# Query, key and value products of an attention block: eight block products or seven, head groups by pairs or segment by segment

## The chip, the cores and the metric

The kernel runs on one core of one Trainium2 chip. A core has five engines that work side by side, each through its own list of instructions in order: TensorE (matmuls, called PE in the profile, its weight loads PEld), VectorE (DVE), ScalarE (ACT), GpSimd (POOL) and SyncE (SP). SP here only issues transfers, which 16 DMA engines carry out. Operands lie in SBUF, an on-chip memory of 128 partitions; matmul results go to PSUM, which has eight banks of 128 x 512 floats. DRAM is outside. An engine waits for another through semaphores. The metric is the device time of one execution in microseconds, lower being better.

## What is computed

A transformer block on 2048 tokens of 1024 features: attention with a compressive memory, then a gated feed-forward, each behind a layer norm whose scale and shift come from a conditioning vector. Cut to what matters:

```python
h = _layernorm(x) * (1 + ca) + sa
q, k, v = h @ wq, h @ wk, h @ wv          # 32 heads of 32, four segments of 512 tokens
for s in range(4):
    p = softmax(qs @ ks.T * scale + causal_mask)      # within the segment
    a_dot = p @ vs
    a_mem = (phi(qs) @ M) / (phi(qs) @ z + 1e-6)      # memory of the segments before
    o = g * a_mem + (1 - g) * a_dot
    M, z = M + phi(ks).T @ vs, z + phi(ks).sum()
x = x + ga * (o @ wo)
h = _layernorm(x) * (1 + cb) + sb
x = x + gb * ((gelu(h @ w_gate) * (h @ w_up)) @ w_down)
```

## The kernel before

Every large product is made in three matmuls: both operands are cut into a high part, which a matmul takes in one pass, and a low part, the rest; high x high, high x low and low x high are added. A cut is one copy on ScalarE and one subtraction on VectorE or GpSimd.

The feed-forward (`gate_up`, L1034, and `down_seven`, L1205) already uses a scheme of seven products in place of eight: both operands are seen as 2 x 2 blocks, sums and differences of blocks are formed, and seven block products, added in the right way, give the four blocks of the result. Its combined weights (tiles `B`, 512 KB with high and low part) are made once, stored in the DRAM tensor `bc_d`, and loaded again for the later token passes (`b_load`, L994).

Attention goes in 32 steps, each for one group of four heads and one segment of 512 tokens. The list `steps` (L1410) takes segments 0 and 1 of all eight groups first, then segments 2 and 3, so that the weights of a group serve two steps. `weights` (L347) loads and cuts them; the normed, transposed tokens of two segments stay in SBUF (`hT_tile`, L73). Inside a step:

- `kv_part` (L423) makes keys and values in ordinary products, tokens by features: 96 matmuls of 256 columns. `k_out` (L386) turns the keys and copies them by three transfers into the stacked tile `ks`: the 128 partitions of four heads become 32 partitions times four, three times over (L395).
- `q_part` (L439) makes the queries in 24 matmuls of 512 columns, and three more transfers stack them in `qs` (L419).
- `scores` (L482) finds each row's maximum and sum: 16 matmuls, each with a VectorE and a ScalarE operation behind it. `sums` and `memory` (L466, L520) carry the memory forward and read it.
- `values` (L544), one step later, makes the transposed scores (`T`), their exponentials, and the product with the values, and stores 256 KB to `oT_d`.

TensorE's order is the program's throughout (`manual_schedule`, L1418), SP's at the start (L1419) and in the feed-forward (L1511); otherwise a planner orders each engine's instructions when the kernel is built, from costs that it assumes. All transfers leave through SP's one queue. The string `ORDER` (L1411) is the interleaving: its letters take one piece each from the generators of values (V), scores (S), memory sums and reads (A, M), keys and values of the next step (K), queries of the next step (Q) and the norm of later tokens (N). In the last steps K and Q stand for the output projection (`projections`, L675). `todo` lists weight loads and modulation rows by position. `first_part` (L450) makes the products of step 0 while the start is still loading.

Of the kernel before, what the change touches and what calls it, by code (L numbers as in the profile page):

```python
# [11 lines left out]
F32 = mybir.dt.float32  # L12
F32R = mybir.dt.float32r
AF = mybir.ActivationFunctionType
ALU = mybir.AluOpType
# [21 lines left out]
def block_kernel(ctx: ExitStack, tc: tile.TileContext, x, c, wmod, wq, wkv, wo, beta, wg, wu, wd, out):  # L37
# [21 lines left out]
    podd, podd_close = pool("podd", "left")  # L59
    pev, pev_close = pool("pev", "left")  # L60
    pw, pw_close = pool("pw", "left")
    pa, pa_close = pool("pa", "right")

# [3 lines left out]
    def wsp_tile(name):  # L67
        return pw.tile([P, 2, 1024], F32R, name=name, tag="wsp", bufs=5)
# [4 lines left out]
    def hT_tile(name, s):  # L73

        return (pev, podd)[s % 2].tile([P, L], F32R, name=name, tag="hT", bufs=16)
# [33 lines left out]
    raw0 = [fetch(wkv[0, 0], "k0"), fetch(wkv[0, 1], "v0"), fetch(wq[0], "q0")]  # L109
# [94 lines left out]

    def load_w(src, name):
        return split_w(fetch(src, name), wsp_tile("w" + name))
# [118 lines left out]
    def norm_seg(s, halves):  # L325
        hs = hT[s] = []
        for kt in range(KT):
            ps = s_ps(f"tpa{s}_{kt}")
            for i in range(4):
                nc.tensor.transpose(ps[:, i * P:(i + 1) * P], halves[kt // 4][i][:, (kt % 4) * P:(kt % 4 + 1) * P], ident)  # L330
            h = tmp_tile(f"h{s}_{kt}")
            nc.scalar.activation(h, ps, AF.Identity, bias=modT[:, kt:kt + 1], scale=modT[:, 8 + kt:9 + kt])
            hi = hT_tile(f"hha{s}_{kt}", s)
            lo = hT_tile(f"hla{s}_{kt}", s)
            nc.scalar.activation(hi, h, AF.Copy)  # L335
            nc.vector.tensor_sub(lo, h, f32(hi))  # L336
            hs.append((hi, lo))
            yield


    hT, W, Mst, ST, SC, PK = {}, {}, {}, {}, {}, {}
    ks_t = []
    for n in range(2):
        k = p1.tile([P, 4, L], F32R, name=f"ks{n}")
        ks_t.append(k)

    def weights(half, g, at):  # L347

        W[g] = [None] * 3
        raws = [None] * 3  # L350

        def get(i):
            raws[i] = fetch((wq[g], wkv[g, 0], wkv[g, 1])[i], f"{i}_{half}_{g}")

        def cut(i):
            W[g][i] = split_w(raws[i], wsp_tile(f"w{i}_{half}_{g}"))

        for pos, f, i in at:
            todo.append((pos, lambda f=f, i=i: (get, cut)[f](i)))

    def kv_mm(ps, g, s, t, kt, **kw):
        hi, lo = hT[s][kt]
# [1186 lines left out]
```

## Time and profile before

| | |
|---|---|
| median of three runs | 2916.93 us (2914.0 to 2917.47) |
| the profiled execution | 2917.27 us, its span 2915.5 us |
| start, to the end of the first products | 0 to 52 us |
| the stretch of the attention products | 52 to 984 us |
| last steps and output projection | 984 to about 1202 us |
| feed-forward | 1202 to 2915 us |
| matmuls of keys and values (L366) | 3072 of 256 columns |
| matmuls of queries (L372) | 768 of 512 columns |
| bytes moved in all | 682.97 MB |

The profile gives busy times per engine; a "chain" follows the last instruction back through what released each step; a table by windows gives busy time, granted TensorE clock, the share of time that the 16 DMA engines were taken, and the rate. For a group of instructions a row holds the line, the engine, the operation, result <- operands, the shape, the count, the busy time in us, the mean duration of one in ns, and the idle time ahead of it. A matmul's duration is its latency; matmuls overlap, so what one costs is read from the distance of their starts, or from a run of them in the chain.

### The profile page before, as it was taken

What the parts mean: (1) busy time and instruction counts of PE and PEld (TensorE: products, weight loads), DVE (VectorE), ACT (ScalarE), POOL (GpSimd) and SP (SyncE); (2) the same over time, 40 slices, a digit from 0 to 9 for tenths busy, and PEclk for the clock granted to TensorE, in tenths of its full rate; (3) what the DMA queues carried; (4) which work ended last, traced back from release to release, by engine and by line L of the source; (5) the groups of instructions that cost most, each with busy time, mean ns of one, the idle gap of its engine ahead of it and who ended that gap; (6) DMA issues with size and microseconds to landing.
All of it is one profiled execution on the core that took longest, in us unless ns stands there. A gap on an engine that the chain in (4) does not pass through costs nothing.

```text
span 2915.5 us, 48821 instructions
## 1 busy us (share of the span) xinstructions
PE 2833.7 (97%) x17248; PEld 2532.0 (87%) x17248; DVE 1860.2 (64%) x4293; ACT 1263.5 (43%) x3112; POOL 882.6 (30%) x1428
## 2 busy tenths in 40 slices
PE   5999999999999999999999999999999999999999
PEld 4788887888888778899999999899999998999998
DVE  7566566766666824656666666756666685666667
ACT  6677776776666624355433333221222122221221
POOL 0333334433343423544455443112211111111111
PEclk9999999999999999999999999999999999999999
DMA  7557656666555648778888776988877788777775
GB/s 241 110 124 138 149 112 132 146 134 121 108 114 95 165 158 263 285 276 307 296 312 322 306 262 242 377 315 308 314 290 281 281 332 308 283 286 289 289 289 210
DMA packets 236053, 682.97 MB, mean 234 GB/s; under 512 B 23712, under 2 KB 62624, under 8 KB 225312
## 3 DMA queue, kind: packets, MB, share of 16 engines
q1 hardware_dynamic: 235808, 679.85, 72.0%
q8 instruction: 136, 2.23, 0.3%
q14 instruction: 109, 0.89, 0.1%
HBM read 454.32 MB, written 175.11 MB: 216 GB/s over the span
## 4 chain that ended last, share of the span: by engine, by line
PE 76%; DVE 8%; DMA 6%; ACT 4%; issue 3%; POOL 2%; SPq 0%; DVEq 0%; POOLq 0%; ACTq 0%
PE f L1043 32%; PE kv L366 9%; PE d L1286 7%; PE y L627 4%; PE q L372 3%; PE T L557 3%; PE db L1223 2%; PE da L1223 2%; PE ds L1223 2%; PE dc L1223 2%; PE S L493 2%; PE O L566 2%; ACT sj L497 2%; DMA B<-bc_d 1%; PE dd L1223 1%
## 5 line engine op out<-in xcount | busy, mean ns | idle before, releaser
L1043 PE MATMUL f<-A,B 128*128 128x320 f32 (+1 forms) x7056 | 1118.3, 319 | 15.7 <-DMA B<-bc_d 9.3
L1043 PEld LDWEIGHTS f<-A,B 128*128 128x128 f32 x7056 | 1104.3, 188 | 24.9 <-DVE c L1055 6.2
L495 DVE CUSTOM_DVE_ANT_0 sj<-S,mask 128x384 f32<-128x384 f32 (+3 forms) x512 | 229.6, 487 | 227.2 <-PE S L493 208.8
L497 ACT ACTIVATE sj<-sj,mm 128x384 f32<-128x384 f32 (+3 forms) x512 | 281.4, 551 | 114.7 <-DVE mm L495 114.4
L789 POOL TENSOR_TENSOR rt<-rt 128x256 f32<-128x256 f32 x104 | 79.0, 781 | 739.6 <-DMA rt<-wd 656.5
L560 POOL TENSOR_SCALAR_AFFINE_SELECT pt<-pt 128x128 f32<-128x128 f32 x512 | 171.0, 355 | 340.2 <-ACT pt L559 334.4
L1286 PE MATMUL d<-wd,hc 128*128 128x512 f32 x1128 | 260.2, 390 | 1.9 <-DVE hc L1106 1.3
L1286 PEld LDWEIGHTS d<-wd,hc 128*128 128x128 f32 x1128 | 211.0, 188 | 46.3 <-DVE hc L1106 2.0
L366 PE MATMUL kv<-w,hha 128*128 128x256 f32 x1024 | 207.4, 288 | 3.4 <-ACT hha L335 3.4
L366 PE MATMUL kv<-w,hhh 128*128 128x256 f32 x1024 | 201.6, 285 | 0.0
L559 ACT ACTIVATE pt<-T 128x256 f32<-128x256 f32 (+3 forms) x512 | 181.7, 456 | 39.0 <-PE T L557 34.4
L202 POOL TENSOR_TENSOR w<-r,w 128x256 fp32r<-128x256 f32 x180 | 133.0, 769 | 166.7 <-ACT w L197 166.5
L366 PEld LDWEIGHTS kv<-w,hha 128*128 128x128 f32 x1024 | 170.0, 195 | 4.7 <-ACT hha L335 4.3
L1115 ACT ACTIVATE hc<-g 128x256 fp32r<-128x256 f32 (+2 forms) x182 | 78.2, 443 | 212.3 <-DVE acc L1232 124.0
L1066 ACT ACTIVATE g<-g 128x320 f32<-128x320 f32 (+1 forms) x84 | 41.1, 489 | 292.3 <-DVE g L1065 292.3
L366 PEld LDWEIGHTS kv<-w,hhh 128*128 128x128 f32 x1024 | 166.4, 191 | 0.3 <-issue 0.2
L1312 DVE TENSOR_TENSOR acc<-acc,d 128x512 f32<-128x512 f32 x176 | 118.8, 684 | 57.5 <-PE d L1286 56.3
L557 PEld LDWEIGHTS T<-qs,ks 128*128 128x128 f32 x512 | 81.2, 191 | 84.7 <-issue 35.1
L366 PE MATMUL kv<-w,hla 128*128 128x256 f32 x512 | 147.6, 288 | 6.8 <-DVE hla L336 6.3
L557 PE MATMUL T<-qs,ks 128*128 128x256 f32 (+2 forms) x512 | 128.6, 361 | 20.2 <-DVE qs L510 7.6
L366 PE MATMUL kv<-w,hlh 128*128 128x256 f32 x512 | 144.9, 283 | 0.0
L1053 ACT ACTIVATE c<-f 128x320 f32<-128x320 f32 (+1 forms) x84 | 38.2, 455 | 236.6 <-PE f L1043 236.6
(246 smaller groups left out, 5247.9 us busy)
## 6 DMA issues: line engine op xcount, KB each, us to landing
B<-bc_d SPq DMA_DIRECT2D x392, 512.0 KB, 6.8
bc_d<-B SPq DMA_DIRECT2D x196, 512.0 KB, 6.7
wd<-wc_d SPq DMA_DIRECT2D x54, 1024.0 KB, 8.1
wc_d<-wd SPq DMA_DIRECT2D x28, 1024.0 KB, 8.0
rt<-wd SPq DMA_DIRECT2D x54, 512.0 KB, 7.5
ks<-kh SPq DMA_DIRECT2D x64, 256.0 KB, 5.6
qs<-qh SPq DMA_DIRECT2D x64, 256.0 KB, 7.3
wm<-wmod SPq DMA_DIRECT2D x32, 512.0 KB, 5.1
```

What stands on the lines that cost most here:

```text
L202: eng.tensor_sub(w[:, 1, k:k + 256], r[:, k:k + 256], f32(w[:, 0, k:k + 256]))
L366: nc.tensor.matmul(ps, b[:, sl], w[:, a], start=(kt == 0 and a == 0 and b is hi), stop=(kt == KT - 1 and a == 1), **kw)
L495: nc.vector.tensor_tensor_reduce(out=sj[:, :nv], in0=ps[:, :nv], in1=mask[:, L - nv:], scale=-1.0, scalar=3.4e38, op0=ALU.add, op1=ALU.min ...
L497: nc.scalar.activation(sj[:, :nv], sj[:, :nv], AF.Exp, bias=mm[:, j, i:i + 1], scale=-1.0, accum_out=ll[:, i, j:j + 1])
L557: nc.tensor.matmul(ps[:, :nn], ks[:, j, kc * P:(kc + 1) * P], qs[:, j, L - nn:], start=True, stop=True)
L559: nc.scalar.activation(pt, ps[:, nn - n:nn], AF.Exp)
L560: nc.gpsimd.affine_select(pt[:, :P], pt[:, :P], pattern=[[1, P]], compare_op=ALU.is_ge, fill=0.0, base=0, channel_multiplier=-1)
L627: nc.tensor.matmul(ps, b[:, i * P:(i + 1) * P], w[:, a, g % 2], start=(g == 0 and a == 0 and b is hi), stop=(g == G - 1 and a == 1))
L1043: nc.tensor.matmul(ps, B[m, i][:, a, kt * P:(kt + 1) * P], A[p, i, kt][b], start=(start and kt == 0 and a == 0 and b == 0), stop=(kt == 3 ...
L1223: nc.tensor.matmul(ps, t[:, c:c + P], B(a), start=(start and a == 0 and b == 0), stop=(stop and a == 1), skip_group_check=True)
L1286: nc.tensor.matmul(ps, hid[m][:, b, tt * P:(tt + 1) * P], down_w[m][:, a, nb * L:(nb + 1) * L], start=(m == chunks[0] and a == 0 and b == ...
L1312: nc.vector.tensor_add(dst, dst, ps)
```

## The change

Attention goes segment by segment: all eight groups of segment 0, then of segment 1 and so on, in alternating order of the groups, so that the last group's weights of one segment serve the first step of the next. Queries and keys of a group are one product of tokens by [wq | wk], values of four groups another; each is done in seven block products, with the two halves of the 512 tokens and of the 1024 features as blocks of the one operand, and of the weights as blocks of the other. The first value products and groups 0 and 1 of segment 0 remain ordinary ones.

```diff
+    ad_d = dram.tile([(NSEG - 1) * 7 * P, 4 * L], F32, name="ad_d")
+    bq_d = dram.tile([G * 7 * P, 2 * L], F32, name="bq_d")
+    bv_d = dram.tile([4 * 7 * P, 2 * L], F32, name="bv_d")
...
+    NB = 9
+    PRODUCTS = (1, 6, 2, 7, 5, 4, 3)
```

The weight combinations of a unit are made once (`make`), each cut and stored as a 512 KB tile; the six units that segment 0 needs next go straight into the pool of nine tiles as well. Afterwards `pump` loads them back in the order of the list `lq`, one for each tile released:

```diff
+    def make(u, jit):
...
+        g, v = (fetch(src, f"{nm}_{k}") for k, src in enumerate(srcs))
...
+        def put(i, src, eng):
...
+            cut(t[:, 0], t[:, 1], src, eng)
+            nc.sync.dma_start(b_rows(u, i), f32(t.rearrange("p a b -> p (a b)")))
+            stored.add((u, i))
...
+    def pump():
+
+        while lq and unmade[0] == 0 and alive[0] < NB and lq[0] in stored:
+            u, i = lq.pop(0)
+            t = B[u, i] = b_tile(f"B{'_'.join(str(v) for v in u)}_{i}_{len(lq)}")
+            nc.sync.dma_start(f32(t.rearrange("p a b -> p (a b)")), b_rows(u, i))
...
+    def release(u, i):
+        del B[u, i]
+        alive[0] -= 1
+        pump()
...
+        for s in range(1, NSEG):
+            for u in units(s)[1:]:
+                lq += [(v, i) for i in PRODUCTS for v in ([u] if u[0] == "q" else [(*u, j) for j in range(2)])]
```

The combinations of the next segment's tokens (`a_forms`) are made on GpSimd and VectorE, stored in `ad_d` in 256 KB pieces, and loaded product by product while the last unit of a segment runs (`a_load`, two transfers for each of seven products). A query-key unit has seven products of 12 matmuls of 256 columns; keys now come out as features by tokens, so they are turned for the memory only (not in the last segment). A value unit, for four groups, has seven products of 24:

```diff
+    def qk_unit(n, g, s, keep, following):
...
+            for kt in range(4):
+                for a, b in ((0, 0), (0, 1), (1, 0)):
+                    nc.tensor.matmul(ps, w[:, a, kt * P:(kt + 1) * P], A_(i, kt, b),
...
+            if not keep:
+                release(u, i)
+            if following:
+                a_load(following, i)
...
+        yield from product(pA, 1, True)
+        nc.scalar.activation(c, pA, AF.Copy)
+        yield from product(pB, 6, True)
+        nc.vector.tensor_add(u2, pB, c)
+        yield from product(pA, 2, False)
+        nc.scalar.activation(qf[:, :HQ], pA, AF.Copy)
+        yield from product(pB, 7, False)
+        nc.vector.tensor_add(kf[:, HQ:], pB, c)
+        pC = mm_ps("pc" + nm)[:, :HQ]
+        yield from product(pC, 5, True)
+        nc.vector.tensor_add(kf[:, HQ:], pC, kf[:, HQ:])
+        yield from product(pB, 4, False)
+        nc.vector.tensor_add(qf[:, HQ:], pB, c)
+        q_out(n, g, s, qf)
+        yield from product(pC, 3, False)
+        nc.vector.tensor_add(kf[:, :HQ], pC, u2)
+        k_out(n, g, s, kf)
```

The six stacking copies of a step stay; those of the keys are put off while the tile they write is still read:

```diff
+        if n < 2 or n - 2 in read:
+            stack()
+        else:
+            stacks[n] = stack
```

The interleaving has letters for the attention parts alone; between them stand pieces of the products ("P"), as many per step as `quota` says. When the products are used up, the pools are closed, the output weights are fetched and cut over the next positions, and the projection follows once they are there:

```diff
-    steps = [(hf, g, s) for hf in range(2) for g in range(G) for s in (2 * hf, 2 * hf + 1)]
-    ORDER = "K N V K V K N K V N V V V K K S K S Q V V V S K A S Q M K Q Q V V"
+    steps = [(n, g, s) for n, (s, g) in enumerate((s, g) for s in range(NSEG) for g in groups(s))]
+    ORDER = "V N M S N V V N S N V V N S N V V S N A V N V V V"
...
+    def quota(n):
+        if n == 0:
+            return 24
+        if n < 7:
+            return 14
+        if n == 7:
+            return 40
+        return 21 if n < 30 else 10 if n == 30 else 24
...
+        return [(0, lambda: get(0)), (2, lambda: get(1)), (6, lambda: cutw(0)), (8, lambda: get(2)), (12, lambda: cutw(1)),
+                (14, lambda: get(3)), (18, lambda: cutw(2)), (22, lambda: cutw(3))]
...
+        elif len(oh[0]) == KT and len(wot[0]) == 4:
+            next(proj, None)
```

At the start `first_part` becomes `rows`: for each of eight feature blocks 12 matmuls of 512 columns for the values of four groups and 6 for queries and keys of group 0, each block's piece behind its two modulation columns. The remaining modulation rows are loaded in steps 12 to 27, two per step.

More of the change, by code (lines that the diff above doesn't have):

```diff
@@ L572, in values @@
             T(kc)
+            if kc == 3:
+                read.add(step)
+                if step + 2 in stacks:
+                    stacks.pop(step + 2)()
             yield
@@ L669, in load_late @@
                 rs[k] = fetch(wo[1, k], f"o1_{k}")
+            while k > 2 and 27 + k not in read:
+                yield
             if k > 0:
```

643 lines of the change are left out of this document (458 added, 185 removed).

## The prediction

> **What bounds the kernel now.** I read the page first: the shares of the engines, and the 40 slices.
>
> ```profile
> span 2915.5 us, 48821 instructions
> PE 2833.7 (97%) x17248; PEld 2532.0 (87%) x17248; DVE 1860.2 (64%) x4293; ACT 1263.5 (43%) x3112; POOL 882.6 (30%) x1428
> DMA  7557656666555648778888776988877788777775
> GB/s 241 110 124 138 149 112 132 146 134 121 108 114 95 165 158 263 285 276 307 296 312 322 306 262 242 377 315 308 314 290 281 281 332 308 283 286 289 289 289 210
> ```
>
> TensorE is busy for 97% of the span. The DMA digits say something less expected: the attention part (slices 2 to 14) holds the transfer engines at 5 to 6 tenths while moving only 95 to 165 GB/s; the feed-forward part moves twice that at 7 to 9 tenths. So attention's transfers are dear for their bytes. The change touches the stretch from the end of the first products (52 us) to the last query product (984 us); here is that stretch, from the table by windows (columns: PE, PEld, DVE, ACT, POOL busy us, clock, DMA share, GB/s), and two pieces of the chain of work inside it.
>
> ```profile
> 52.00:984.00 932.00, 901.77 (x6467) 761.47 (x6466) 606.07 (x2011) 654.63 (x1852) 329.26 (x724) 0.99 0.62 126
> ```
>
> ```profile
> 413.46 2.87 PE kv L366 x24
> 428.18 2.76 PE q L372 x12
> ```
>
> TensorE works 902 of 932 us, and the DMA engines are taken for 0.62 x 932 = 578 us. A 256-column product matmul costs 2.87/24 = 0.1196 us, a 512-column one 2.76/12 = 0.230 us: time goes by columns, so fewer columns do save time.
>
> **What it takes from TensorE.** Before: 32 steps of 96 matmuls of 256 columns (keys and values) and 24 of 512 (queries): 3072 x 0.1196 + 768 x 0.230 = 544 us. After: 30 query-key units of 84 and 6 value units of 168, all of 256 columns, and in segment 0 still 192 + 96 ordinary ones of 512: 3528 x 0.1196 + 288 x 0.230 = 488 us. Saved: 56 us, not an eighth of 544 (68), since part of segment 0 stays ordinary. Key transposes go for the last segment only:
>
> ```profile
> L390 PE MATMUL kT<-ident,kn 128*128 128x128 f32 x128 | 19.8, 276 | 2.7 <-ACT kn L383 2.7
> ```
>
> A quarter of 19.8 is 5 us at most; I take 4. The first products now take 18 matmuls of 512 per feature block in place of 12 of 256 and 3 of 512: 8 x (4.14 - 2.13) = 16 us more at the start, partly under the waits for modulation columns; I take 13, so the stretch begins at 65 us. TensorE's need in it: 902 - 528 (products in it before) + 455 (488 less the 33 of the first products) - 4 = 825 us. If nothing else binds, this is the gain.
>
> **What it adds to the transfers.** Here the matter is decided. First the prices, from four stretches and the issues of SP in one of them:
>
> ```profile
> 22.00:32.00 10.00, 8.12 (x37) 7.25 (x38) 10.00 (x21) 6.07 (x7) 0.00 (x0) 1.00 1.02 408
> 402.00:419.00 17.00, 15.99 (x120) 13.30 (x119) 9.75 (x26) 9.45 (x30) 9.06 (x20) 1.00 0.88 195
> 433.00:443.00 10.00, 10.00 (x81) 8.23 (x80) 2.91 (x6) 6.01 (x18) 5.03 (x16) 1.00 1.08 128
> 1820.00:1895.00 75.00, 68.75 (x395) 63.95 (x394) 57.10 (x109) 22.86 (x53) 8.67 (x10) 0.98 0.99 372
> ```
>
> ```profile
> 400.43 0.33 SPq L184 DMA_DIRECT2D wm<-wmod  x1
> 400.85 1.20 SPq L396 DMA_DIRECT2D ks<-kh  x2
> 404.38 0.55 SPq L396 DMA_DIRECT2D ks<-kl  x1
> 405.02 0.55 SPq L420 DMA_DIRECT2D qs<-qh  x1
> 407.62 0.55 SPq L420 DMA_DIRECT2D qs<-ql  x1
> 408.22 0.60 SPq L420 DMA_DIRECT2D qs<-qh  x1
> 408.87 0.58 SPq L592 DMA_DIRECT2D oT_d<-R  x1
> 409.55 0.40 SPq L99 DMA_DIRECT2D r<-wq  x1
> 410.05 1.46 SPq L184 DMA_DIRECT2D wm<-wmod  x1
> ```
>
> Plain loads of 512 KB fill the engines at 408 GB/s: 1.29 us each. Loads and stores of such operands mixed, in the feed-forward part, run at 372: 1.41 us. But at 433 to 443, where almost nothing but the six stacking copies of a step runs (128 to 32 partitions, 256 KB each), the engines are full at 128 GB/s: 2.05 us per copy. At 402 to 419 they stand among three loads and a store: 0.88 x 17 = 15.0 us, less 3 x 1.29 + 0.70, leaves 10.4 for six, 1.73 us each.
>
> Nor do other transfers pass them. The six copies and the output store of a later step, as SP issues them, and the load behind them there and in the chain of work:
>
> ```profile
> 457.75 1.21 SPq L396 DMA_DIRECT2D ks<-kh  x2
> ...
> 463.60 0.54 SPq L592 DMA_DIRECT2D oT_d<-R  x1
> 464.56 15.09 SPq L99 DMA_DIRECT2D r<-wkv  x2
> ```
>
> ```profile
> 464.56 9.30 DMA r<-wkv
> ```
>
> Issuing this pair held SP for 15 us, and the load is 9.3 us of the chain. So I treat the engines as one resource on which times add up. The stretch after the change needs:
>
> - reloaded operands: segments 1 to 3 each fetch 7 products x (7 query-key units + 2 x 2 value halves) = 77 tiles of 512 KB; 231 x 1.41 = 326 us
> - their stores: 12 units x 7 = 84 x 1.41 = 118 us
> - raw weights 28, modulation rows 32, tokens 12: 72 x 1.29 = 93 us (raw weights were 45)
> - 256 KB pieces at 372 GB/s (0.70): 32 outputs, 24 stores and 36 reads of the normed tokens, 84 stores of token combinations: 124 us
> - reloading these combinations: 42 x 1.41 = 59 us
> - the copies, unchanged: 192 x 1.73 = 332 us
>
> Sum: 1052 us, against TensorE's 825. The copies' price is the unknown: in a queue that is never empty they may mix better. Its ends are 2.05 (alone) and 0.64 (bytes at 408 GB/s); I take the mixed row, 1.73.
>
> The Trainium skill bears on this price: SBUF — State Buffer, section "Door 1: The DMA port swizzle", says that partitions 0 to 31 reach only 8 of 16 ports and gives 189 to 218 GB/s for them. The trace is slower still, 128 GB/s. By the page's rate the copies would be an estimated 231 to 266 us and the sum 951 to 986.
>
> The same prices applied to the stretch before (186 copies, 87 loads, 46 pieces, 8 reloads) give 322 + 112 + 32 + 11 = 477 us, where the row shows 578: the prices are rather low than high.
>
> **Sum.** The stretch ends at 65 + 1052 = 1117 us in place of 984: +133. Then the end of attention: products run out in step 30, and only then are the output weights fetched and cut, so one and a half steps have no matmuls between their softmax parts. ScalarE needs 654.63/32 = 20.5 us per step, TensorE's own part is (902 - 528)/32 = 11.7: 1.5 x 8.8 = 13 us. The rest (projection, feed-forward) keeps its operations. 2917.27 (the profiled execution: 2915.5 of span and 1.8 around it) + 133 + 13 = 3063. The median, 2916.93, is 0.3 lower; **I forecast 3063 us.**
>
> The cuts and additions cost nothing in this sum: they lie under the wait for transfers. Nearest rows (one instruction, mean ns):
>
> ```profile
> L539 DVE TENSOR_TENSOR ry<-num,dn 128x256 f32<-128x256 f32 x34 | 12.7, 414 | 0.0
> L409 ACT ACTIVATE qh<-q 128x512 fp32r<-128x512 f32 x21 | 12.4, 589 | 6.3 <-PE q L372 6.2
> L202 POOL TENSOR_TENSOR w<-r,w 128x256 fp32r<-128x256 f32 x128 | 94.7, 770 | 111.9 <-ACT w L197 111.7
> ```
>
> Segment 0 makes all 84 operands: 84 x 0.589 = 49 us more on ScalarE, 12 x 12 x 0.77 = 111 us on GpSimd. ScalarE then has 8 x 20.5 + 49 + 18 (token combinations, other cuts) = 231 us in segment 0, over TensorE's 195 there (33 + 60 of products, 8 x 11.7, norms) but under the transfers' (118 of stores, 36 of weights, 48 copies 83, some 50 of tokens: 287). If transfers didn't bind, this would cost up to 30 us. VectorE gains five 256-column additions per unit (5 x 0.41 = 2.1 us) on 606/32 = 19 per step, and stays below the step.
>
> **Rivals.**
>
> *TensorE stays the bound (faster).* If copies cost no more than their bytes, the transfers are 720 + 123 = 843 us, as much as TensorE's 825. For it: at 372 GB/s the stretch 1820 to 1895 still has TensorE at 92%. Against it: it is not full there, and the wait list of that stretch names the loaded operand:
>
> ```profile
> PE f L1043 <- DMA B<-bc_d: 4.7, 2, 3.8
> ```
>
> Time: 65 + 843 = 908, that is 76 less, plus 13, plus 20 of segment 0: about 2875 us.
>
> *The copies mix halfway.* At 1.2 us, between 0.64 and 1.73, the transfers are 950 us: +31 + 13, 2961 us. The row at 433 to 443 speaks against it, the full queue for it. The page's port rule would put the result here. At 1.0 it is 2923, hardly to be told from no change: 0.2% (6 us) is about what a measurement of this kernel can tell.
>
> *SP holds the queue empty (slower still).* SP has one list (inside attention a planner's), and a copy waiting in it for its source holds the loads behind it:
>
> ```profile
> SPq L396 <- ACT ek L400: 88.7, 7, 22.1
> SPq L396 <- ACT kh L393: 51.9, 10, 6.8
> ```
>
> That is 141 us of SP waiting in 600 (300 to 900 us). Behind it would now stand the reloads, nine tiles ahead of TensorE. It decides where a wait outlasts what is queued, some 8 transfers as at 464 us, or 12 us; the longest is 22. A tenth of the stretch empty: +105, 3168 us. Against it: the change puts off copies whose destination is still read.
>
> **Chances and range.** Transfers bind at about the priced sum (2990 to 3130): 0.50. Copies mix: 0.14 slower by a few per cent, 0.06 no change. TensorE binds, 2850 to 2910: 0.22. SP's order, above 3130: 0.08. So faster 0.22, same 0.06, slower 0.72. The forecast's own range is 2990 to 3130; to hold 8 in 10 with the other side it reaches from 2865 to 3150.
>
> **What would show it.** Right: DMA share above 0.9 from 65 to beyond 1080 us at 290 to 340 GB/s; TensorE below 85% there, its waits led by the loaded operands B and by work behind the copies; query-key matmuls still at 0.12 us when they run. Wrong: a DMA share near 0.8 with TensorE above 95%, the copies well above 128 GB/s in effect. Then the price of the copies is the failed term. If segment 0 alone is long while segments 1 to 3 keep TensorE full, the making of operands bound it, not the reloads.

## The result, and the profile after

| | before | after |
|---|---|---|
| median | 2917.09 us (4 runs) | 3361.57 us (3359.93 to 3375.34, 4 runs) |
| ratio | | 1.1537, 95% interval 1.1505 to 1.1568 |
| end of the product stretch | 984 us | 1396 us |
| first matmul of the feed-forward | 1192 us | 1640 us |

The changed kernel is slower, as forecast, but by 445 us where 146 were forecast; the time lies outside the range. The page of the changed kernel, its shares and some of its 40 slices:

```profile
span 3360.9 us, 50067 instructions
PE 2911.1 (87%) x17192; PEld 2555.9 (76%) x17192; DVE 1987.4 (59%) x4526; ACT 1324.2 (39%) x3282; POOL 924.0 (27%) x1488
PE   6645646877887788799999999999999999999999
PEclk8777778989998999899999999999999999999999
DMA  8577889889899998747878797769788779876775
GB/s 251 141 231 227 235 262 296 245 243 257 255 256 257 273 251 246 169 136 233 279 289 326 276 341 286 264 267 375 281 327 321 270 271 340 331 291 257 288 297 217
```

TensorE is no longer full in the first half, and the transfer engines are mostly at 7 to 9 tenths there, not at 10. No engine is full: something makes them take turns. The table by windows of the changed kernel, cut where the scores of a segment begin, and at the end of the products (columns as in the prediction):

```profile
68.00:544.00 476.00, 254.57 (x1523) 211.18 (x1523) 213.79 (x572) 225.51 (x601) 190.03 (x324) 0.75 0.76 226
544.00:869.00 325.00, 258.35 (x1770) 209.35 (x1769) 181.08 (x590) 178.04 (x514) 62.29 (x163) 0.92 0.91 249
869.00:1193.00 324.00, 255.86 (x1775) 206.45 (x1774) 191.41 (x618) 176.93 (x513) 62.97 (x164) 0.93 0.92 261
1193.00:1396.00 203.00, 170.33 (x1242) 136.82 (x1241) 127.38 (x426) 114.58 (x342) 31.59 (x98) 0.99 0.88 241
1396.00:1640.00 244.00, 223.66 (x1019) 171.84 (x1018) 111.23 (x230) 97.85 (x232) 94.47 (x132) 0.92 0.61 188
```

Share times length gives the transfer engines' own time: 362 + 296 + 298 + 179 = 1135 us, against the 1052 forecast. So the sum was 83 us low, no more; but the stretch lasted 1328 us, and the engines stood idle for some 193 of them. Held against the prediction's parts:

| part | forecast | measured | off |
|---|---|---|---|
| start | 65 | 68 | +3 |
| segment 0 (transfers the longest, 287) | 287 | 476 | +189 |
| segments 1 to 3 (1052 - 287) | 765 | 852 | +87 |
| end of the products to the feed-forward (207.7 + 13) | 221 | 244 | +23 |
| feed-forward | 1724 | 1721 | -3 |

What TensorE waited for, in segment 0 and then in segments 1 and 2 of the changed kernel (us in total, times, longest us), from the list of waits:

```profile
PE S L798 <- DMA ks<-kl: 95.1, 6, 38.3
PE pa L642 <- ACT Bq L352: 36.2, 2, 21.1
PE S L798 <- DMA rf<-hT_d: 21.0, 1, 21.0
...
PE S L798 <- DVE mm L800: 43.5, 55, 3.3
PE S L798 <- DMA ks<-kl: 26.8, 5, 10.7
PE S L798 <- DMA Bq<-bq_d: 19.5, 4, 10.2
PE T L865 <- ACT pt L867: 18.3, 39, 1.2
```

These are two different ailments. In segment 0 there are few and long waits, for copies and for operands that are being made. In segments 1 and 2 the largest entry is 55 short waits of the scores (S) for VectorE, with the like of them for ScalarE at the transposed scores (T). Transfers have no part in those, and the kernel before had next to none of either; its first entry between 344 and 809 us:

```profile
PE T L557 <- DVE qs L510: 5.4, 8, 1.2
```

### The profile page after: what moved, and what is told of

Its sections match the earlier page's. It is cut to its first block, busy times and chain, and to the rows that moved or that the text cites. A ratio compares the mean times of both kernels' runs of the same rounds, so it can differ in the third digit from the quotient of the medians.

```text
span 3360.9 us, 50067 instructions
## 1 busy us (share of the span) xinstructions
PE 2911.1 (87%) x17192; PEld 2555.9 (76%) x17192; DVE 1987.4 (59%) x4526; ACT 1324.2 (39%) x3282; POOL 924.0 (27%) x1488
## 4 chain that ended last, share of the span: by engine, by line
PE 61%; DMA 12%; DVE 8%; ACT 5%; issue 3%; POOL 3%; SPq 1%; DVEq 0%; ACTq 0%; POOLq 0%
PE f L1358 28%; PE d L1601 6%; PE y L940 4%; DMA ks<-kl 3%; PE pb L642 2%; PE db L1538 2%; PE da L1538 2%; PE ds L1538 2%; PE dc L1538 2%; ACT sj L802 2%; PE T L865 2%; PE pv L684 2%; PE O L874 2%; DVE sj L800 1%; PE S L798 1%
## 5 line engine op out<-in xcount | busy, mean ns | idle before, releaser
L798 PE MATMUL S<-ks,qs 96*128 96x256 f32 (+2 forms) x512 | 153.9, 388 | 252.3 <-DMA ks<-kl 124.0
L798 PEld LDWEIGHTS S<-ks,qs 96*128 96x128 f32 x512 | 91.8, 210 | 301.4 <-issue 176.8
L865 PE MATMUL T<-qs,ks 128*128 128x256 f32 (+2 forms) x512 | 153.9, 392 | 81.9 <-ACT pt L867 31.7
L865 PEld LDWEIGHTS T<-qs,ks 128*128 128x128 f32 x512 | 96.2, 213 | 120.9 <-ACT pt L867 52.7
L642 PE MATMUL pb<-a,Bq 128*128 128x256 f32 x1080 | 173.0, 302 | 8.9 <-DVE u L660 3.2
L642 PEld LDWEIGHTS pb<-a,Bq 128*128 128x128 f32 x1080 | 150.9, 203 | 32.4 <-issue 19.3
L684 PE MATMUL pv<-Bv,a 128*128 128x256 f32 x1008 | 155.1, 301 | 20.6 <-DMA Bv<-bv_d 19.6
L684 PEld LDWEIGHTS pv<-Bv,a 128*128 128x128 f32 x1008 | 138.9, 203 | 35.8 <-issue 23.3
L1381 ACT ACTIVATE g<-g 128x320 f32<-128x320 f32 (+1 forms) x84 | 41.1, 489 | 291.6 <-DVE g L1380 291.6
L642 PE MATMUL pa<-a,Bq 128*128 128x256 f32 x720 | 117.6, 304 | 36.6 <-ACT Bq L352 36.2
L642 PEld LDWEIGHTS pa<-a,Bq 128*128 128x128 f32 x720 | 101.6, 204 | 52.9 <-ACT Bq L352 37.8
```

The costliest lines, as they stand in the source:

```text
L642: nc.tensor.matmul(ps, w[:, a, kt * P:(kt + 1) * P], A_(i, kt, b), start=(start and kt == 0 and a == 0 and b == 0), stop=(kt == 3 and a == 1),
L684: nc.tensor.matmul(ps[:, tb * HQ:(tb + 1) * HQ], A_(i, kt, b)[:, tb * P:(tb + 1) * P], w[kt // 2][:, c, kt % 2 * HQ:(kt % 2 + 1) * HQ], st ...
L798: nc.tensor.matmul(ps[:, :nk], qs[:96, j, i * P:(i + 1) * P], ks[:96, j, :nk], start=True, stop=True)
L865: nc.tensor.matmul(ps[:, :nn], ks[:, j, kc * P:(kc + 1) * P], qs[:, j, L - nn:], start=True, stop=True)
```

## The experiments

The runs in one table. Steps are the mean distance, in us, of the first transposed scores from one step to the next, by eight steps; the last column is the end of the product stretch. In the kernel before, and so in e4 and e17, the four columns are steps 0 to 7, 8 to 15 and so on, and no segments: its first sixteen steps go through segments 0 and 1 in turn, the others through 2 and 3.

| run | us | segment 0 | 1 | 2 | 3 | products end |
|---|---|---|---|---|---|---|
| before | 2917 | 30.9 | 29.2 | 28.9 | 30.3 | 984 |
| after | 3362 | 56.6 | 41.1 | 39.7 | 35.5 | 1396 |
| e1 copies by ScalarE's queue | 3447 | 55.7 | 44.8 | 43.7 | 39.4 | 1476 |
| e2 half of each reload | 3322 | 55.5 | 38.9 | 36.9 | 36.2 | 1350 |
| e3 four copies of six | 3308 | 54.6 | 38.2 | 38.0 | 35.4 | 1338 |
| e4 before, with 352 more transfers | 2935 | 30.5 | 30.1 | 29.0 | 31.6 | 991 |
| e5 three units made, not twelve | 3268 | 45.4 | 41.0 | 39.7 | 35.5 | 1301 |
| e6 token combinations once | 3310 | 56.2 | 37.4 | 36.6 | 36.0 | 1342 |
| e7 light: e2, e5 and e6 | 3206 | 44.2 | 37.0 | 36.0 | 36.2 | 1235 |
| e8 query copies put off | 3351 | 56.1 | 40.4 | 38.9 | 36.0 | 1382 |
| e9 groups in halves | 3368 | 53.6 | 40.9 | 40.2 | 37.5 | 1399 |
| e10 the same, light | 3210 | 41.7 | 37.8 | 37.0 | 37.3 | 1252 |
| e11 transposed scores first | 3444 | 56.1 | 45.3 | 44.1 | 37.9 | 1478 |
| e12 the same, light | 3227 | 40.4 | 38.8 | 39.3 | 37.1 | 1258 |
| e13 two buffers for ry | 3314 | 56.7 | 38.8 | 39.4 | 31.7 | 1359 |
| e14 the same, light | 3108 | 43.6 | 33.2 | 32.8 | 30.5 | 1154 |
| e15 e13 and another order | 3313 | 56.5 | 38.1 | 39.5 | 32.0 | 1353 |
| e16 the same, light | 3116 | 44.5 | 32.5 | 33.5 | 30.9 | 1166 |
| e17 before, memory part early | 3100 | 33.6 | 33.8 | 38.6 | 37.4 | 1166 |
| e18 e13 and e8 | 3273 | 56.4 | 37.1 | 36.3 | 31.4 | 1322 |

The times of e1 to e8 are single executions, the others medians.

### Is it the transfers?

**e1** sends the six stacking copies by ScalarE's queue, so that they no longer stand in SP's list:

```diff
-                nc.sync.dma_start(f32(ks_t[n % 2][32 * qd:32 * qd + 32]), f32(srct))
+                nc.scalar.dma_start(f32(ks_t[n % 2][32 * qd:32 * qd + 32]), f32(srct))
```

> The six stacking copies of a step leave through ScalarE's list in place of SP's; nothing else changes. Theory T (time on the transfer engines): their sum stays at about 1134 us in the stretch 68 to 1396, so segments 1 to 3, where the engines are taken for 0.91 of 857 us, can't fall below some 780; only segment 0 (354 us of transfers in 471) can give back its waits. 3250 to 3360 us. Theory O (the order of SP's list: copies stand behind stores and loads that wait for something): the waits for the copies go in every segment, 3150 to 3220 us with products ending before 1250.

3447 us, 86 slower than the changed kernel, which neither theory asked for. ScalarE's own list is in order too, and it is on the path of every step; in this run's list of waits it stands still for a copy:

```profile
ACT sj L802 <- DMA ks<-kh: 48.1, 4, 15.5
```

The 86 us were not taken apart further.

**e2** reloads only the high part of each combined weight, and uses it in place of the low part.

```diff
-            nc.sync.dma_start(f32(t.rearrange("p a b -> p (a b)")), b_rows(u, i))
+            nc.sync.dma_start(f32(t[:, 0]), b_rows(u, i)[:, :L])
```

> The reloaded weight tiles of segments 1 to 3 bring only their high part, 256 KB in place of 512 (the low part of the weights is left out of the seven-product units; the matmuls stay as many). Theory T: 231 x 0.70 = 163 us less on the transfer engines, all of it in segments 1 to 3, where they bind: 3180 to 3220 us. Theory O: the list and its waits are the same, only single transfers are shorter: 3300 to 3350 us.

3322 us. At the prediction's price 231 x 1.41 / 2 = 163 us of transfers are gone, and 39 us of time. The transfer engines now have room, and still a step does not fall below 36 us. The window of this run over segment 2:

```profile
836.00:1140.00 304.00, 249.75 (x1778) 200.69 (x1776) 191.42 (x617) 176.20 (x513) 61.66 (x164) 0.96 0.84 212
```

**e3** leaves out two of the six copies (their rows are filled with zeros).

> Two of the six stacking copies of a step are left out, and with them the product of the queries' low part (GpSimd fills those rows with zeros). Theory T: 64 x 1.75 = 112 us less on the engines, 84 of it in segments 1 to 3: 3250 to 3290 us. Theory O: the four that are left stand behind the same transfers: 3320 to 3355 us. If a copy's real price were its bytes (0.64 us), the loss would be 41 us and the time 3320.

3308 us: 64 x 1.73 = 111 us of transfers gone, 53 of time: about a half, where e2 gained a quarter. The engines' own time to the end of the products is 0.80 x 1270 = 1016 us, some 115 less than in the changed kernel, or about 1.8 us a copy. So the price that the prediction called the unknown was right.

**e4** adds to the kernel before 352 transfers of 512 KB, DRAM to DRAM, spread over its attention steps, that nobody waits for.

> The kernel before, with 11 copies of 512 KB between DRAM tensors in each of its 32 steps (352 in all, wanted by nobody, waiting for nothing); products, cuts and order are those of before. At 1.4 to 2 us each they add 490 to 700 us to the 578 us of transfers in its stretch of 932. Theory T: the stretch becomes 1070 to 1280 us and the kernel 3060 to 3270. Theory O: transfers that wait for nothing block little: 2920 to 2980 us.

2935 us, and the window over its product stretch:

```profile
52.00:984.00 932.00, 898.96 (x6437) 759.22 (x6435) 571.60 (x1980) 648.57 (x1834) 306.30 (x710) 0.99 0.98 306
```

The share rose from 0.62 to 0.98: 335 us for the 329 of them that were issued in this stretch, 1.02 each. The sum, 578 + 335 = 913, still fits in 932, so this does not refute adding up. It does show that transfer engines at 0.98 need not slow TensorE (899 us busy, 902 before), and that 0.85 as in the changed kernel is not a full queue.

### Is it the making of operands?

**e5** makes three of the twelve weight units and loads their tiles for all others. **e6** forms the token combinations for one segment and loads them for all. **e7**, the light kernel, does both and takes e2's half reloads.

```diff
-        maker = chain(*(make(u, u in jit) for u in (("q", 2), ("v", 1, 0), ("q", 3), ("v", 1, 1), *jit[2:],
-                                                    ("v", 0, 0), ("v", 0, 1), ("q", 1), ("q", 0))))
+        maker = chain(*(make(u, u in jit) for u in (("q", 2), ("v", 1, 0), ("v", 1, 1))))
```

> Three weight units are made in place of twelve (one query-key unit and the two value halves); the tiles of the others are left out, and wherever they are wanted the stored tiles of the made ones are loaded. Segment 0 took 471 us, with the engines taken for 354. Theory M (making: raw loads, differences, cuts and stores pass one after the other through four shared buffers, and the attention's instructions stand behind them in every engine's list): segment 0 falls to about 290 us, 3361 - 180 = 3180. Theory T (time on the transfer engines): 112 us of making less, 49 us of loads more, so -63: 3300 us.

> The token combinations are made and stored for segment 1 alone; segments 2 and 3 load those of segment 1 again (their own are left out). Theory M: segments 1 and 2, 40.5 us per step, come down to what segment 3 shows, 33.6 us, 2 x 8 x 6.9 = -110: 3250 us. Theory T: 28 stores and 8 reads of 256 KB less per segment, 25 us each: 3310 us.

> Both edits together, and the reloads bring only the high part: making, combinations and half the reloaded bytes are left out. The engines then need about 1134 - 63 - 50 - 180 = 840 us. Theory T: the stretch of products falls to TensorE's need, 830 to 860 us: 2870 to 2900. Theory M with T: the same. Theory P (TensorE waits step by step for VectorE and ScalarE, because the attention's pieces have less product work between them): 30 to 33 us per step stay, a stretch of 960 to 1060 us: 3000 to 3100.

e5: 3268 us, 94 less, nearly all of it in segment 0; the same window in that run:

```profile
68.00:453.00 385.00, 238.66 (x1522) 201.35 (x1523) 166.48 (x526) 190.75 (x538) 105.46 (x216) 0.79 0.80 223
```

385 us in place of 476. So the making of the operands is about half of what the forecast missed in segment 0. The edit takes transfers away as well: the engines' own time there falls from 362 to 308 us, their idle time from 114 to 77. How the 91 us divide between the two is not shown. The list of waits of SP in segment 0 of the changed kernel suggests how making costs beyond its transfers: the stores of finished operands stand in SP's one list until VectorE has cut them, and stacking copies stand behind them.

```profile
SPq L473 <- DVE Bq L357: 56.3, 21, 8.8
SPq L473 <- DVE Bv L357: 28.2, 11, 4.5
```

e6: 3310 us, 52 less, in segments 1 and 2, as theory T asked for. e7: 3206 us, far above the 2870 to 2900 that either main theory asked for, and above the 3000 to 3100 of the third. With light transfers and little making a step still takes 36 us. Its window over segment 2, and what TensorE waits for in segments 1 and 2:

```profile
769.00:1057.00 288.00, 244.05 (x1756) 197.47 (x1755) 177.19 (x588) 161.67 (x474) 38.52 (x134) 0.98 0.78 189
```

```profile
PE S L802 <- DVE mm L804: 42.4, 62, 1.9
PE T L869 <- ACT pt L871: 21.3, 43, 2.8
```

A third bound lies just under the transfers, and so halving a transfer could never show its full price. The Trainium skill (Perfetto Trace Analysis, "Optimization Strategy" under "Identifying Performance Opportunities") says that the same gap repeating on the engine that should be full can mean that a buffer is short in SBUF or PSUM. These 105 gaps are such a row; which buffer it is, they do not say.

### What is the floor of 36 us?

**e8** puts the query copies off as the change does with the keys', so that SP does not wait at them.

> The three copies of the queries are put off like those of the keys, until the transposed scores of two steps before are done; the work is the same. Theory O (order of SP's list): SP waits 86 us at these copies for TensorE, with the reloads behind it; that goes: 3280 to 3320 us. Theory T and theory M: within 20 us of 3361.

3351 us: small.

The timeline of e7 shows a pattern: of each group of four T or S matmuls the first two or three run, and the rest wait until an operation on another engine frees a PSUM bank.

```profile
1106.44 0.52 PE L869 MATMUL T<-qs,ks 128*128 128x256 f32 x3
1107.50 0.39 PE L869 MATMUL T<-qs,ks 128*128 128x256 f32 x1 [0.54 <-ACT pt L871]
```

My first reading was that too little product work stands between the groups, and the second that the new order leaves the key copies too little room: in the trace, from the last T of a step to the first S two steps on (which needs the tile that T read) there are 32 us on average before, and 20 after (S of steps 8 to 31).

**e9** and **e10** issue the groups in halves, two matmuls at a time, in the full and the light kernel:

```diff
+                if j == 1:
+                    yield
...
-    ORDER = "V N M S N V V N S N V V N S N V V S N A V N V V V"
+    ORDER = "V N S V M S N V S N V V S V N S V V N S V S N V V S N A V N V V V"
```

> The changed kernel with the score and transposed-score groups cut in two: two matmuls instead of four between product pieces, the letters of the step's order written anew so that halves of the two alternate; all work stays. P (the groups of four, set with only one or two product pieces of six matmuls between them, wait for the five score banks of PSUM, and that is the floor of some 36 us a step that stayed when transfers were light): segments 1 to 3 come down by 3 us a step, transfers take over part of the gain: 3285 us (3260 to 3310). W (the waits for banks only move, as VectorE's and ScalarE's way from one group to the next is what lasts): 3330 to 3390.

> The same cut of the groups in the light kernel of e7 (three units made, token combinations once, half of each reload; there 36 us a step in segments 1 to 3 and 3206 us). P: 30 to 32 us a step in segments 1 to 3, 3080 us (3050 to 3120), waits of scores for VectorE and of transposed scores for ScalarE under 1 us a step together (2.9 before). W: 35 us a step or more, 3170 to 3240.

3368 us (ratio 1.1561, 1.1543 to 1.1578) and 3210 us (1.1016, 1.0996 to 1.1035). The bank waits went (S for VectorE 42 us in e7, 3 in e10), and the time stayed: now S waits for the key copies instead.

```profile
PE S L802 <- DMA ks<-kl: 37.9, 10, 6.2
```

**e11** and **e12** move the scores behind the transposed scores, as in the kernel before:

```diff
+    ORDER = "V M N V N V V N V V N S N V V S N V S N A S N V V"
```

> The changed kernel with only the letters of a step's order moved: the transposed scores of the step before come first, the scores of the step come in the middle of it, as they stood in the kernel before; all work and all transfers stay. Q (the key copies of a step may start only when the transposed scores two steps back have read their tile, and the new order leaves them some 0.6 of a step until the scores want them, where the old one left a whole step): the scores' waits for the key copies go nearly (19 us in all or less in segments 1 to 3, from about 43), a step of segments 1 to 3 comes from 39 to 36 us or less, 3361 becomes 3270 (3220 to 3300), the rest held by transfers. T (the transfers' sum alone sets the steps): 3340 to 3380.

> The same order in the light kernel of e7 (three units made, token combinations once, half of each reload; 36 us a step in segments 1 to 3, 3206 us). Q: 29 to 32 us a step in segments 1 to 3, 3070 us (3030 to 3110). Rival (the floor is neither the order nor the transfers but product units that wait on their own additions and cuts): 35 us or more a step, 3180 to 3240.

3444 us (1.1804, 1.1780 to 1.1828) and 3227 us (1.1066, 1.1047 to 1.1085). The key copies' waits are gone, as expected, and the time is not: e11 is even 82 us slower than the changed kernel, which neither theory asked for. The scores now end too close to the next step's T, and the bank waits stay; TensorE in segments 1 and 2 of e12:

```profile
PE T L869 <- DVE qs L819: 49.4, 15, 4.5
PE S L802 <- DVE mm L804: 29.8, 61, 1.6
PE T L869 <- ACT pt L871: 15.8, 49, 0.5
```

Each edit took one wait away and met the next. What they had in common was only seen by asking who holds the five score banks of PSUM. The memory part `num` uses two of them; they are read into the tile `ry`, which has one buffer, and the `ry` of the step before is read by the transposes `Y`. In the kernel before (timeline of TensorE, then of VectorE):

```profile
655.75 1.07 PE L531 MATMUL num<-mz,pq 128*128 128x132 f32 x8
659.86 0.60 PE L582 MATMUL Y<-ident,ry 128*128 128x128 f32 x4
```

```profile
662.08 0.75 DVE L539 TENSOR_TENSOR ry<-num,dn 128x256 f32<-128x256 f32 x2
```

In the changed kernel:

```profile
905.67 1.06 PE L836 MATMUL num<-mz,pq 128*128 128x132 f32 x8
943.86 0.60 PE L895 MATMUL Y<-ident,ry 128*128 128x128 f32 x4
```

```profile
944.49 0.76 DVE L844 TENSOR_TENSOR ry<-num,dn 128x256 f32<-128x256 f32 x2 [0.36 <-PE Y L895]
```

`ORDER` now has M third, and Y is still next to last. So from 907 to 945 us two of five banks are taken by results that cannot be read out, and all sixteen S and twelve of the sixteen T matmuls of the step share the other three. Over the 24 steps with memory the hold, from the end of the first `num` matmul to the end of the second read-out, is 7.4 us on average before and 34.4 after.

**e13** and **e14** give `ry` two buffers, in the full and the light kernel. Part of the room for it comes from dropping the constant tile `blk` and letting `tt` share a buffer with `mz`; order and transfers stay.

```diff
-            ry = t2("ry" + nm, "ry", shape=(P, 4, 4, DH))
+            ry = [t2(f"ry{nm}_{i}", "ry", bufs=4, shape=(P, 2, 4, DH)) for i in range(2)]
```

> The changed kernel with a second buffer for ry (room made by dropping one constant tile and sharing another), so that the memory part's two score banks are free after some 3 to 8 us in place of 34; order, transfers and work unchanged. B (the held banks make the floor): waits of scores and transposed scores for VectorE and ScalarE fall by two thirds, a step of segments 1 to 3 by 2 to 4 us, 3361 becomes 3290 (3260 to 3320), more than this being held by transfers. K (with the banks free the scores only wait earlier and longer for the key copies): 3330 to 3380.

> The same second buffer in the light kernel of e7 (three units made, token combinations once, half of each reload; 36 us a step, 3206 us). B: 31 to 33 us a step in segments 1 to 3, 3110 us (3080 to 3140). K: 35 us a step or more, the scores' waits for key copies above 2 us a step, 3170 to 3220.

3314 us (1.1368, 1.1341 to 1.1394) and 3108 us (1.0671, 1.0655 to 1.0687): both inside what the held banks asked for, outside what the copies did. The hold is 2.9 and 2.7 us. In the light kernel this one buffer is worth 3206 - 3108 = 98 us, 33 us a step in place of 36 to 37; in the full one it is worth 48. The full kernel with two buffers, its four segments:

```profile
68.00:538.00 470.00, 250.03 (x1516) 207.57 (x1517) 206.30 (x567) 225.21 (x601) 190.06 (x324) 0.75 0.76 228
538.00:847.00 309.00, 244.65 (x1778) 208.67 (x1776) 181.54 (x596) 174.24 (x514) 62.93 (x163) 0.91 0.92 260
847.00:1168.00 321.00, 243.51 (x1773) 209.17 (x1774) 190.44 (x618) 172.84 (x513) 61.71 (x164) 0.89 0.94 265
1168.00:1359.00 191.00, 167.55 (x1239) 141.67 (x1240) 126.95 (x421) 112.40 (x341) 32.27 (x98) 0.96 0.94 257
```

and the light one:

```profile
68.00:445.00 377.00, 239.20 (x1523) 200.41 (x1523) 173.01 (x525) 189.90 (x538) 103.77 (x216) 0.81 0.71 192
445.00:704.00 259.00, 233.97 (x1768) 202.00 (x1767) 171.91 (x575) 163.55 (x486) 39.12 (x135) 0.95 0.80 194
704.00:974.00 270.00, 238.31 (x1775) 205.43 (x1774) 182.13 (x601) 163.68 (x485) 39.67 (x136) 0.94 0.83 205
974.00:1154.00 180.00, 163.68 (x1246) 139.52 (x1245) 128.30 (x428) 112.04 (x342) 30.48 (x98) 0.98 0.77 174
```

Segments 1 and 2 take 630 us with full transfers and 529 with light ones, segment 0 470 against 377. In segments 1 and 2 of the full kernel the buffer is worth 19 us only (649 to 630), since the transfers come next there, at 0.92 to 0.94, as the forecast had them. The rest comes elsewhere: 6 us in segment 0, 12 in segment 3 (203 to 191) and 17 behind the products (244 to 227), less 4 that the feed-forward is longer.

**e15** and **e16** add to this an order with the transposed scores first and the scores done six product pieces before the step's end.

> The second ry buffer, and transposed scores first, scores in the middle third of the step and done some six product pieces before its end; all work stays. B and K together (banks and the room for key copies make the floor): room from the last transposed score to the scores two steps on near 30 us (20 before), a step of segments 1 to 3 at 36 us or less, 3250 us (3200 to 3290). If transfers alone set the full kernel's steps: 3330 or more.

> The same two edits in the light kernel. B and K together: 29 to 31 us a step in segments 1 to 3, 3050 us (3010 to 3090), TensorE busy above 95 per cent there. If something else makes the floor: 34 us a step or more, 3150 or more.

3313 us (1.1372, 1.1355 to 1.1389) and 3116 us (1.0701, 1.0683 to 1.0719): both between what their two theories asked for, and no gain over e13 and e14, though the room for the key copies rose to 39 and 34 us. With the banks free the room was not a bound. In segments 1 and 2 of e15 TensorE's waits are now led by loaded operands, the sign that the prediction had named for bound transfers:

```profile
PE pa L640 <- DMA a<-ad_d: 26.1, 4, 7.4
PE pv L682 <- DMA Bv<-bv_d: 25.7, 9, 4.6
```

**e17** moves the letter M in the kernel *before* from behind the scores to the step's start.

```diff
-    ORDER = "K N V K V K N K V N V V V K K S K S Q V V V S K A S Q M K Q Q V V"
+    ORDER = "K N V M K V K N K V N V V V K K S K S Q V V V S K A S Q K Q Q V V"
```

> The kernel before with one letter moved: the memory part of a step is issued near the step's start, as in the changed kernel, in place of after the last scores; ry keeps its one buffer, so two of five score banks are held until the transposes Y near the step's end (some 25 us a step in place of 7). Nothing else changes. B (held banks alone make a floor): 24 steps at 32 to 33 us in place of 29, 2995 us (2975 to 3030). Rival (the wider pieces of product work, 12 matmuls or 1.4 us, cover the three banks that remain): under 2945.

3100 us (1.0642, 1.0626 to 1.0658): one letter costs 187 us, more than either theory asked for. But it is not the banks. Of this run's 24 memory parts the first 8, those of segment 1, hold their banks for some 3 us (the step before has no memory yet, so no `ry` is waiting); the other 16 hold theirs for some 33. The lengths of the steps, by the segment of the memory part that falls in them (means of seven, first transposed scores to the next):

| segment | 0, no memory part | 1, short hold | 2, long hold | 3, long hold |
|---|---|---|---|---|
| before | 30.4 | 29.8 | 29.2 | 29.0 |
| e17 | 29.7 | 37.7 | 38.5 | 37.8 |

So 8 us a step come with the memory part's early place alone. With the long hold it is 9, so here the hold is worth about 1 us a step (1.4 at most, in segment 2). Part of the 8 us is another wait: `num` now waits for VectorE's work on the queries, which this order makes at the end of the step before (TensorE, 344 to 984 us; in all `num` stands still for 3.8 us a step):

```profile
PE num L533 <- DVE pq L418: 39.3, 11, 6.2
```

The rest was not taken apart. So the rival's time is missed, but this run does not refute what it says of the banks: in the kernel before, banks held for 33 us make hardly any floor. In the changed kernel e13 and e14 show that they cost. That the wider pieces of product work make the difference, as the rival has it, was not tried.

**e18** adds e8's putting off of the query copies to e13, which left SP waiting 62.8 us in segments 1 and 2 for T before it could issue them.

> The changed kernel with the second ry buffer (e13, 3314 us) and the query copies put off until their destination is free, like the keys' (e8). In e13 the transfer list waits 63 us in segments 1 and 2 for the transposed scores before it can issue query copies, with the engines at 0.93. O (that order costs): 3280 us (3265 to 3295), the transfer engines' share there at 0.96 or more. T (the sum of transfers sets these segments): 3300 to 3320.

3273 us (1.1231, 1.1212 to 1.1251): 41 us less than e13. The same edit gave 10 while the banks were held. Its windows:

```profile
68.00:543.00 475.00, 255.62 (x1521) 212.14 (x1522) 214.59 (x569) 225.42 (x601) 190.33 (x324) 0.74 0.75 226
543.00:838.00 295.00, 242.66 (x1772) 206.58 (x1771) 180.46 (x593) 174.22 (x514) 60.84 (x163) 0.93 0.96 273
838.00:1136.00 298.00, 242.68 (x1775) 208.08 (x1775) 191.30 (x618) 173.12 (x513) 61.59 (x164) 0.91 0.96 284
1136.00:1322.00 186.00, 166.34 (x1241) 140.98 (x1240) 127.68 (x424) 112.10 (x340) 32.26 (x98) 0.96 0.95 264
```

From segment 1 on the engines are at 0.95 to 0.96: this is the state that the prediction had described, and these segments take 779 us where it had said 765. It is the best full version of the change found, and 358 us of span slower than the kernel before: 200 of them in segment 0, 122 in segments 1 to 3, 16 at the start and 20 behind the products (68, 475, 779 and 228 us, against 52, 275 for the first eight steps, 657 and 208).

## Why the prediction was right and wrong

**Slower, and by transfers: right in part.** The sum was 1052 us and the engines took 1135 (that the prices were rather low, the prediction had seen on the kernel before: 477 us for 578); in e18, with the held banks and the waiting query copies out of the way, segments 1 to 3 take 779 us for a sum of 765.

**The step that failed** is "So I treat the engines as one resource on which times add up", when it was carried over into "The stretch ends at 65 + 1052 = 1117 us": it took the longest resource for the time. That holds only if nothing holds the transfers up. The engines were busy for 0.85 of the stretch (1135 of 1328 us); 193 us of idle time and 83 of a sum set too low make the 276 that are missing there. What held them up stood in the order of the work, which the sum leaves out.

- *The order inside a step.* The prediction counted every operation and transfer of the change, and passed over the new `ORDER`. It moved the memory part from behind the scores to the step's start, and so turned a hold of two PSUM banks from 7.4 into 34.4 us. What it costs is shown by e14 (98 us) and e13 (48 us). The hold was to be seen beforehand: one buffer for `ry`, M and Y as letters of a string, and five score banks. Its price was not: in the kernel before nearly the same hold costs about 1 us a step (e17).
- *Segment 0.* "The cuts and additions cost nothing in this sum: they lie under the wait for transfers" is the step that fails here: 476 us for 287. Of the 189 that are missing 75 are transfers (362 for 287; 22 reloaded weight tiles and 14 loads of token combinations, 36 x 1.41 = 51 us, already run in this segment) and 114 are idle time of the transfer engines. The prediction compared the busy times of engines there (ScalarE 231, TensorE 195, transfers 287) and took the largest. None was full: ScalarE was busy 226 of 476 us, the transfer engines 0.76. Making an operand is a chain of load, differences, cut and store, and its stores stand in the same list as the stacking copies. e5 takes 91 us away with nine of twelve units. The other half of the 189 stays open; in e5 TensorE's waits there are led by transfers of tokens (`rf<-hT_d` 34.6 us, `hT_d<-hta` 21.0) and of keys (25.0), and none of these was tried.

Of the 299 us between forecast and result the buffer is worth 48, the query copies put off behind it 41, and the making, on its own, 94. The remaining 116 are open, most of them in segment 0, and whether the three add up was not tried.

**The rivals.** "TensorE stays the bound" and "copies mix halfway" fall. "SP holds the queue empty" was the nearest, at 0.08: waits in SP's list do empty the queue. It was put at a tenth of the stretch and 3168 us; the idle share was 0.15. Its reason against, that the change puts off copies whose destination is still read, holds for the keys only; putting off the queries' too gave 41 us in e18.

**Single terms.** Product matmuls of 256 columns still run at some 0.12 us where nothing slows them (six in 0.72 us, 910.90 to 911.62). The start was 3 us late. The end of attention cost 36 us more than before where 13 were taken: the term was too small. The second buffer takes 17 of the 36 away; the rest was not tried. "If segment 0 alone is long while segments 1 to 3 keep TensorE full, the making of operands bound it" was half the sign: segment 0 was long, and TensorE was not full in the others either.

**The range** had its upper end at 3150, and the one rival above it, the starved queue, was priced at 3168. A change that rewrites the order of a tuned interleaving has an unknown cost of its own, and no row of the trace of before bounded it; the range should have said so.

## What to carry to other kernels

When a change rewrites the order of pieces, follow each buffer that has one or two copies through the new order: who writes it, who reads it last, and what is held in between. A late reader can lock PSUM banks for a whole step, and the list of waits shows it only as many short waits of other matmuls. Whether the lock costs anything depends on what still has to pass through the other banks (98 us in e14, about 1 us a step in e17).

When an experiment removes a cost and gains a fraction of it, look for a second bound just underneath, and remove both at once: e2, e5 and e6 together gave 156 us, the buffer alone 48, and all four together 253, some 50 more than the sum of the two.

The longest resource is a lower bound of a stretch, not its time; look at the lists in which unlike work stands in one line (here SP's), and at what stands at their head.

## What the runs showed of the hardware

Transfers can fill the 16 engines to 0.98 of 932 us beside TensorE at 0.96 (e4) without slowing it by more than 17 us in the whole kernel.

In these rows TensorE's granted clock goes with the length of the waits rather than with their number. In segment 2 of e7, with over a hundred waits for banks in two segments and none above 3.2 us, it is 0.98; in e14, with fewer waits but some of 4.5 us, 0.94; in segments 1 and 2 of the changed kernel, with waits up to 10.7 us, 0.92 and 0.93; in its segment 0, with waits up to 38, 0.75. The Trainium skill (TensorE: Matmul & The Clock Gate, "HAM oscillation — how this bites in real kernels") puts the limit at idle gaps of some 3.4 us. In these runs shorter waits are enough, though not each time: in e7 TensorE waits 1.90 us for a bank, and in the 3.4 us behind it the clock is at 0.51. Six product matmuls take 0.79 us before that wait and 1.28 behind it, so a wait can be paid more than once.

```profile
519.97 0.55 PE L802 MATMUL S<-ks,qs 96*128 96x256 f32 x1 [1.90 <-DVE mm L804]
```

```profile
520.00:523.40 3.40, 3.40 (x16) 3.40 (x17) 0.72 (x7) 2.63 (x10) 0.00 (x0) 0.51 0.35 112
```

Behind a wait of 1.88 us at 818.8 us of the same run it stays at 1.00. The Trainium skill says in the section after that one ("A second HAM failure mode: psum-queue depth-cycling") that cycling through PSUM banks lowers the clock too. With its hundred waits at banks e7 still has 0.97 and 0.98 in segments 1 and 2, so here the effect is small at most. In the eight steps of e17 with the banks held, and then in the same eight of the kernel before, nearly the same count of matmuls takes 14% more busy time:

```profile
635.00:944.00 309.00, 259.31 (x1665) 208.91 (x1664) 153.07 (x524) 162.49 (x457) 82.60 (x189) 0.93 0.46 92
```

```profile
578.00:809.00 231.00, 227.76 (x1664) 192.55 (x1663) 151.54 (x523) 158.65 (x456) 82.55 (x190) 1.00 0.61 121
```

How much of this is the clock, and how much is the time in which a waiting matmul is counted as busy, these rows do not tell.
